# Attention's products with V in four array quadrants, and six blocks turned for the gate by transfers

## Chip, cores, metric

The kernel runs on one core of a Trainium2 chip. The metric is the device time of one launch in microseconds (us), the median of several runs; lower is better. Engines are named as in the profile: PE (TensorE's matmuls), PEld (its weight loads), DVE (VectorE), ACT (ScalarE), POOL (GpSimd) and SP (SyncE, which issues most transfers here). Matrix data are fp32, and an fp32 matmul with 65 moving columns leaves two records of each kind (LDWEIGHTS, MATMUL) in the trace.

## What is computed

Local and global attention over 4 sequences of 768 tokens with 8 heads of 64, then a mixture of 8 experts, of which each token takes two.

```python
scores = scale * q @ k.T + bias          # kept: the first 8 keys, and the 96 last ones up to the token
a = softmax(scores)                      # (B, H, S, S), masked
x = (a @ v).transpose(0, 2, 1, 3).reshape(3072, 512)
noisy = x @ w_gate + log1p(exp(x @ w_noise)) * noise
# the two best experts of each token, weighted by the softmax of their two values
out[t] += weight[t, e] * (relu(x[t] @ w1[e]) @ w2[e])
```

## The kernel before

**Attention** goes over 24 blocks of 128 tokens (`g`; six to a sequence, `i` counts them within it). A loop of 48 iterations takes four heads of a block each; `n` steps by 2, so iteration k has n = 2k and each block has two. Keys of a block are a window: 96 of the block before, 8 global ones and the block's own, and the 128 queries are dealt with in two halves `s` of 64, each with a window of 168 keys (`WIN`). The schedule is written out by hand, and each engine runs its instructions in that order. One iteration does, in this order: `score(n + 2)` (four DVE operations that read the scores' banks, four exponentials on ACT), `trans(n)` and `trans(n + 1)` (six PE transposes, two copies on ACT), in every second iteration `gate_t` of an earlier block, then `product(n + 4)` (eight PE matmuls of 64x64 weights in four quadrants of the array, rows by head, columns by `y`), `norm(n - 4)` (three DVE operations that read the PSUM bank of an earlier product with V), `attend(n - 2)` (the product with V), parts of the gate, and what is due by `todo` (loads of q, k and v three blocks ahead, w1 of the first expert split into two parts by ACT and POOL, zeroing). Iteration 10 forms the first scores of block 6, iteration 12 those of block 7.

**attend** (L859). In a block with i > 0 it has 16 matmuls in two rounds of eight. In round 0, weights of 64 rows sit at array position (0, 0) for one half of the queries and of 40 rows at (64, 64) for the other, so two quadrants work. In round 1, weights of 104 and 128 rows take the whole height, in two column halves. Each matmul moves 65 columns (64 of V and a column of ones, for the softmax's sum). One call writes one PSUM bank, and calls alternate between banks 5 and 6 (`rings`), so `norm` of one call reads a bank that the next `attend` does not write.

**V** is loaded by `load_v` (L657): `vs`, 128 rows of 2080 bytes, and for i > 0 `vp`, 96 rows of the block before and 8 global rows (the latter only in the first four uses of each sequence's buffers, as a transfer of its own).

**The gate** needs each block's x with features along the partitions. `gate_t` (L365) copies x on POOL into two planes of 16-bit halves (`halved`, four copies of 128x256), which `gate_l` (L382) has SP store to DRAM (`xd`) for the later gathers; it turns x by four PE transposes into bank 2, and ACT copies the 128x512 result into `pair` (L380). `gate_l` multiplies two blocks at a time with the gate's weights, `gate_s` brings the result into place, and `route`, a chain of small DVE steps dealt out by `tick`, chooses experts after blocks 5, 11, 16, 20 and 23.

**Experts** follow. The first begins with `turn` of its gathered tokens and `up(0, ...)`, the others run the same way, and in them tokens are turned by SP's transposing transfer and joined by ACT (`flip` L260, `weave` L269). PSUM bank tags 5 and 6 serve `down` there.

SP issues its transfers in program order.

Of the kernel before, what the change touches and what calls it, by code (L numbers as in the profile page):

```python
# [10 lines left out]
F32 = mybir.dt.float32  # L11
# [10 lines left out]
P = 128  # L22
# [13 lines left out]
def tile_local_global_attention_then_moe(  # L36
# [24 lines left out]
    NT = B * NB  # L61
    WIN = NP + NG + Q
    windowed = 1 <= n_local <= NP + 1 and 0 <= n_global <= NG
    scale = 1.0 / math.sqrt(D)
# [15 lines left out]
    turns = {}  # L80

    def bank(tag):
        ring = rings[tag]
        key = tuple(ring)
        turns[key] = turns.get(key, -1) + 1
        return psum.tile([P, 512], F32, name=tag, tag=f"b{ring[turns[key] % len(ring)]}", bufs=1)

# [271 lines left out]
    def partner(g):  # L359
# [3 lines left out]
        return (g - a) % 2  # L363

    def gate_t(g):  # L365
        x = XR.pop(g).rearrange("p h d -> p (h d)")
        stored[g] = gp.tile([P, 2 * Dm], U16, name="xt", bufs=4)
        halved(planes(stored[g]), words(x))
        ps = bank("m").rearrange("p (k t) -> p k t", k=KC)
        for k in range(KC):  # L370
            nc.tensor.transpose(ps[:, k], x[:, k * P:(k + 1) * P], ident)
        j = partner(g)
        if j is None:
            XT[g] = ys[2].rearrange("p (k t) -> p k t", k=KC)
            to = XT[g]
        else:
            if j == 0:
                XT[g + 1] = pairs[0].rearrange("p (k j t) -> p k j t", k=KC, j=2)
            to = XT[g + 1 - j][:, :, j]
        nc.scalar.activation(to, ps, AF.Copy)  # L380

    def gate_l(g):  # L382
        nc.sync.dma_start(xd[DUMP + g * P:DUMP + (g + 1) * P], stored.pop(g))
        j = partner(g)
        if j == 0:
            return
        ps = bank("m")[:, :P]
        x = XT.pop(g)
        x = [x] if j is None else [x[:, :, i] for i in range(2)]
# [243 lines left out]
    with ExitStack() as actx:  # L633
        ac = actx.enter_context(tc.tile_pool(name="ac", bufs=1))
        aw = actx.enter_context(tc.tile_pool(name="aw", bufs=2))

        qs, ks, vs, vp = {}, {}, {}, {}
# [19 lines left out]
        def load_v(g):  # L657

            b, i = divmod(g, NB)
            vs[g] = aw.tile([P, HD], F32, name="vs", bufs=4)  # L660
            nc.sync.dma_start(vs[g], v[b, i])
            if i:
                vp[g] = vpb[g % 4]
                nc.sync.dma_start(vp[g][:NP], v[b, i - 1, P - NP:])
                if i <= 4:
                    nc.sync.dma_start(vp[g][NP:], v[b, 0, :NG])

        if windowed:
            vpb = [ac.tile([NP + NG, HD], F32, name=f"vp{j}") for j in range(4)]
            pairs.append(ac.tile([P, 2 * Dm], F32, name="pair"))  # L670
# [52 lines left out]

            abuf = [ac.tile([P, 2 * WIN], F32, name=f"a{j}") for j in range(4)]
        else:
# [121 lines left out]
        def trans(n):  # L847
            g, u, b, i = geo(n)
            w = 3 * P if i else 2 * P
            ps = bank("at")[:, :w]  # L850
            x = A.pop(n)
            for k, c in enumerate((0, 2 * WIN - P, NP + NG) if i else (0, P)):
# [6 lines left out]
        def attend(n):  # L859

            g, u, b, i = geo(n)
            ps = pav[g, u // 2] = bank("av")[:, :4 * D1].rearrange("p (h d) -> p h d", h=4)
            at = [AT.pop(n + x) for x in range(2)]
            heads = [(at[x], 2 * y + x, y * Q) for x in range(2) for y in range(2)]
            parts = [[(vs[g], 0, P, 0)], [(vs[g], 0, P, 1)]]
            if i:
                parts = [[(vs[g], 0, Q, 2), (vp[g], 0, NP + NG, 0)], [(vp[g], Q, NP + NG, 2), (vs[g], 0, P, 1)]]
            n = len(parts[0])
            for k in range(n):
                for a, h, q0 in heads:  # L870
                    c = slice((u // 2 * 4 + h) * D1, (u // 2 * 4 + h + 1) * D1)
                    for s in range(2):
                        t, r, z, part = parts[s][k]
                        nc.tensor.matmul(ps[s * Q:(s + 1) * Q, h], a[r:z, part * P + q0:part * P + q0 + Q], t[r:z, c],  # L874
                                         start=k == 0 and (n == 1 or h == 0), stop=k + 1 == n,
                                         tile_position=(r, s * Q), skip_group_check=True)

        def norm(n):
# [3 lines left out]
            if u == 0:  # L882
                XR[g] = ys[g % 2].rearrange("p (h d) -> p h d", h=H)
            den = aw.tile([P, 4], F32, name="den", bufs=2)
            nc.vector.tensor_scalar(den, ps[:, :, D], 1e-9, None, op0=OP.add)
            tick(4)
            nc.vector.reciprocal(den, den)
            tick(5)
            h0 = 2 * u
# [11 lines left out]
        def whole(g):  # L901
# [20 lines left out]
            for hp in range(HP):  # L922
# [8 lines left out]
                for x in range(2):  # L931
# [13 lines left out]
                    for j in range(NB):  # L945
# [10 lines left out]
                                     den[:, :, None].to_broadcast([P, 2, D]))  # L956
            for f in gate_t, gate_l, gate_s:
                f(g)
# [20 lines left out]
        else:  # L979
# [27 lines left out]
            for n in range(0, NPAIR, 2):  # L1007
# [40 lines left out]
            for t in range(TA):  # L1048
                if t == 2:
                    gate_l(NT - 2)  # L1050
                turn(0, t, bank("sc"))
# [7 lines left out]

    rings.update(sc=[0, 1], m=[2])  # L1060
    with ExitStack() as mctx:
        mc = mctx.enter_context(tc.tile_pool(name="mc", bufs=1))
        w2h = mc.tile([P, FC, Dm], FR, name="w2h")
# [116 lines left out]
        def back(e, i):  # L1180
# [11 lines left out]

        late, last = pending
        slots = {
            0: [(late, 24)], 1: [gate_t, (late, 27)], 2: [(late, 30)], 3: [gate_l, (late, 33)],
            4: [(late, 36)], 5: [gate_s, (late, 39)], 6: [(late, 42)], 7: [(late, 45), (last, 2)],
            8: [], 9: [(late, 48), (last, 5)], 10: [(last, 7)], 11: [(last, 8)],
            12: [(late, 52), (last, 9)], 13: [(last, 12)], 14: [(last, 14)], 15: [(late, 54), (last, 16)],
            16: [(last, 19)], 17: [(last, 21)], 18: [(last, 23)], 19: [(last, 26)],
            20: [(last, 30)], 21: [(last, 33)], 22: [(late, 57), (last, 35)], 23: [(last, 37)],  # L1200
            24: [(last, 39)], 25: [(last, 42)], 26: [(late, 61)], 27: [(last, 45)],
            28: [(last, 48)], 29: [(late, 99), split], 30: [split], 31: [(last, 52)],
        }
# [290 lines left out]

    wctx.close()
    left = nc.values_load(more[0:1, E:E + 1], min_val=0, max_val=N)
    with tc.If(left > 0), tc.tile_pool(name="lc", bufs=1) as lc:
# [92 lines left out]
```

## Time and profile before

| | us |
|---|---|
| median of 3 runs (lowest, highest) | 720.09 (717.33, 720.92) |
| the profiled execution, device time | 718.65 |
| its span, first to last instruction | 716.9 |
| PE busy in the span | 692.7 |
| DVE / ACT / POOL busy | 457.1 / 440.0 / 323.3 |
| mean granted clock of PE | 0.995 of 2.4 GHz |

The profile is of one execution. "Busy" is the union of an engine's instructions; matmuls overlap in the array, so PE is busy for nearly the whole span and this alone doesn't say how well it is used. The chain of waits follows the work that ended last backwards; an operation whose share of it is large sets the time in that stretch. Attention takes roughly the first 160 us of the span.

### The profile page before, as it was taken

What the parts mean: (1) busy time and instruction counts of PE and PEld (TensorE: products, weight loads), DVE (VectorE), ACT (ScalarE), POOL (GpSimd) and SP (SyncE); (2) the same over time, 40 slices, a digit from 0 to 9 for tenths busy, and PEclk for the clock granted to TensorE, in tenths of its full rate; (3) what the DMA queues carried; (4) which work ended last, traced back from release to release, by engine and by line L of the source; (5) the groups of instructions that cost most, each with busy time, mean ns of one, the idle gap of its engine ahead of it and who ended that gap; (6) DMA issues with size and microseconds to landing.
All of it is one profiled execution on the core that took longest, in us unless ns stands there. A gap on an engine that the chain in (4) does not pass through costs nothing.

```text
span 716.9 us, 16231 instructions
## 1 busy us (share of the span) xinstructions
PE 692.7 (97%) x5769; PEld 618.3 (86%) x5769; DVE 457.1 (64%) x1473; ACT 440.0 (61%) x922; POOL 323.3 (45%) x416
## 2 busy tenths in 40 slices
PE   7999999999999799999999999999999999999995
PEld 5888888787789699999799989999899898889984
DVE  7669888977946376746564665576376756656600
ACT  6888787662437496546664685587467646755511
POOL 3363626481087362164606462644555344632222
PEclk9999999999999999999999999999999999999999
DMA  8996778685098784167916792587459547843233
GB/s 252 336 279 216 216 233 289 203 299 188 0 261 181 155 141 118 27 120 160 207 16 133 158 217 48 118 174 165 75 148 201 108 121 166 185 74 89 31 45 47
DMA packets 129913, 111.10 MB, mean 155 GB/s; under 512 B 51578, under 2 KB 96762, under 8 KB 129824
## 3 DMA queue, kind: packets, MB, share of 16 engines
q1 hardware_dynamic: 118416, 83.84, 42.9%
q0 software_dynamic: 11264, 25.89, 20.1%
q8 instruction: 47, 0.77, 0.5%
q14 instruction: 42, 0.34, 0.2%
q10 hardware_dynamic: 144, 0.26, 0.1%
HBM read 71.07 MB, written 27.59 MB: 138 GB/s over the span
## 4 chain that ended last, share of the span: by engine, by line
PE 64%; DVE 10%; issue 8%; DMA 7%; POOL 5%; ACT 5%; POOLq 0%; SPq 0%; ACTq 0%; DVEq 0%
PE bank L1397 20%; PE av L1144 19%; PE av L1167 7%; PE av L874 4%; PE sc L823 4%; PE at L853 3%; DMA xt<-xg 3%; DMA xg<-xd,ids 2%; DVE wall L196 2%; PE at L1107 1%; ACT hh L1088 1%; DVE w2l L196 1%; POOL out_dram L1120 1%; DVE ns L837 1%; DMA xd<-xt 1%
## 5 line engine op out<-in xcount | busy, mean ns | idle before, releaser
L1397 PE MATMUL bank<-xh,wall 128*128 128x384 f32 (+4 forms) x784 | 216.3, 343 | 1.1 <-ACT aside L1438 0.9
L1397 PEld LDWEIGHTS bank<-xh,wall 128*128 128x128 f32 x784 | 143.5, 188 | 6.7 <-DVE wall L196 1.4
L1397 PE MATMUL bank<-xl,wall 128*128 128x384 f32 (+4 forms) x392 | 133.4, 340 | 0.0
L1144 PE MATMUL av<-w2h,hh 128*128 128x512 f32 x304 | 120.3, 396 | 4.0 <-ACT aside L1176 2.3
L1120 POOL DMA_INDIRECT out_dram<-y,ids x40 | 63.8, 1596 | 127.7 <-ACT y L1117 124.4
L1144 PE MATMUL av<-w2h,hl 128*128 128x512 f32 x304 | 119.5, 393 | 0.3 <-DVE hl L1092 0.3
L1144 PE MATMUL av<-w2l,hh 128*128 128x512 f32 x304 | 119.1, 392 | 0.0
L196 DVE TENSOR_TENSOR wall<-raw,wall 128x512 fp32r<-128x512 f32 (+1 forms) x84 | 73.0, 875 | 48.4 <-ACT wall L195 48.3
L1092 DVE SCALAR_TENSOR_TENSOR hl<-bank,hh 128x384 fp32r<-128x384 f32 (+4 forms) x84 | 47.1, 561 | 66.5 <-ACT hh L1088 66.3
L195 ACT ACTIVATE wall<-raw 128x512 fp32r<-128x512 f32 (+1 forms) x84 | 58.0, 698 | 43.2 <-POOL raw L1252 43.2
L243 POOL DMA_INDIRECT xg<-xd,ids x53 | 58.8, 1109 | 52.1 <-DVE place L293 32.5
L840 ACT ACTIVATE a<-ns,mx 128x168 f32<-128x168 f32 (+1 forms) x192 | 67.9, 422 | 19.3 <-DVE mx L837 18.6
L1397 PEld LDWEIGHTS bank<-xl,wall 128*128 128x128 f32 x392 | 73.9, 188 | 2.7
L275 ACT ACTIVATE xg<-xt 128x1024 uint16<-128x1024 uint16 (+3 forms) x46 | 60.0, 1307 | 19.7 <-DMA xt<-xg 19.6
L1144 PEld LDWEIGHTS av<-w2h,hl 128*128 128x128 f32 x304 | 57.1, 188 | 14.1 <-DVE hl L1092 1.5
L1144 PEld LDWEIGHTS av<-w2h,hh 128*128 128x128 f32 x304 | 57.1, 188 | 14.0 <-ACT aside L1176 2.5
L1144 PEld LDWEIGHTS av<-w2l,hh 128*128 128x128 f32 x304 | 57.1, 188 | 9.3 <-DVE w2l L196 0.3
L837 DVE CUSTOM_DVE_ANT_0 ns<-sc,bias 128x168 f32<-128x168 f32 (+1 forms) x188 | 51.7, 319 | 18.4 <-PE sc L823 12.3
L1251 POOL TENSOR_TENSOR raw<-raw 128x256 f32<-128x256 f32 x28 | 21.9, 781 | 85.8 <-DVE wall L196 85.4
L874 PE MATMUL av<-vs,at 128*64 128x65 f32 (+1 forms) x768 | 57.3, 224 | 0.0
L235 POOL COPY xt<-y 128x256 uint16<-128x256 uint16 x96 | 35.2, 405 | 49.0 <-DVE y L890 46.9
L1088 ACT ACTIVATE hh<-bank 128x384 fp32r<-128x384 f32 (+4 forms) x84 | 41.8, 497 | 23.6 <-DVE bank L1467 16.0
(214 smaller groups left out, 1485.6 us busy)
## 6 DMA issues: line engine op xcount, KB each, us to landing
raw<-in_w SPq DMA_DIRECT2D x64, 256.0 KB
raw<-in_w SPq DMA_DIRECT2D x32, 512.0 KB
out_dram<-zero SPq DMA_DIRECT2D x14, 512.0 KB
vs<-in_v SPq DMA_DIRECT2D x24, 260.0 KB
xd<-xt SPq DMA_DIRECT2D x24, 256.0 KB
qbuf<-in_q SPq DMA_DIRECT2D x23, 256.0 KB
ks<-in_k SPq DMA_DIRECT2D x20, 272.0 KB
vp<-in_v SPq DMA_DIRECT2D x20, 195.0 KB
```

Of the source, the lines that this page charges most:

```text
L195: nc.scalar.activation(hi, src, AF.Copy)
L196: eng.tensor_sub(lo, src, hi.bitcast(F32))
L243: nc.gpsimd.indirect_dma_start(out=xg[e, t].bitcast(U16)[:m], out_offset=None, in_=xd[:n], in_offset=bass.IndirectOffsetOnAxis(ap=r, axis= ...
L275: nc.scalar.activation(words(x), xt.pop((e, t)).rearrange("p (h k) t -> p h (k t)", h=2), AF.Copy)
L837: nc.vector.tensor_tensor_reduce(out=ns[x][:, s, :w], in0=ps[:, s], in1=bias[:, u + x, s] if i else bias0[:, u + x, s], scale=-scale, scal ...
L840: nc.scalar.activation(A[n + x][:, s * w:(s + 1) * w], ns[x][:, s, :w], AF.Exp, bias=mx[x][:, s:s + 1], scale=-1.0)
L874: nc.tensor.matmul(ps[s * Q:(s + 1) * Q, h], a[r:z, part * P + q0:part * P + q0 + Q], t[r:z, c], start=k == 0 and (n == 1 or h == 0), stop ...
L1088: nc.scalar.activation(inner(e)[0][j][:, f, :src.shape[1]], src, AF.Relu)
L1120: ins = nc.gpsimd.indirect_dma_start(out=out, out_offset=bass.IndirectOffsetOnAxis(ap=r, axis=0), in_=y, in_offset=None, bounds_check=N + ...
L1144: nc.tensor.matmul(ps, x[j][:, f, cols], w[:, f], start=n == 0, stop=n == 3 * FC - 1)
L1167: nc.tensor.matmul(to, w[:, f, cols], x[:, f], start=n == 0, stop=n == 3 * FC - 1)
L1397: nc.tensor.matmul(ps, wb[c % 2][u][:, 2 * a + k], x[v][:, 2 * b + k], start=start and n == 0, stop=stop and n == 5, skip_group_check=True)
```

## The change

Two parts. `attend` keeps its 16 matmuls, but round 0 is dealt over four quadrants: of heads with x = 0 as before, of heads with x = 1 at (64, 0) and (0, 64). To this end the attention weights of odd heads are laid out in another order in their buffer (24 columns longer, the first 24 of them zero, by two memsets), V comes from the host in two arrangements, one for even and one for odd heads, and `vp` is a full 128-row transfer (260 KB, one transfer instead of one or two). Heads with x = 0 and x = 1 write different banks, so each call writes both banks of one tile `av` (`P, 2, 512`), in one of three column ranges in turn; `norm` reads both banks.

For blocks 0, 1, 2, 3, 8 and 9 (`LATE`), `gate_t` only makes the 16-bit planes; `store` has SP store them, and then turns them with a transposing transfer into `flipped`; `gate_w`, one block later, joins the planes on POOL (four copies of 128x256) into a tile of its own; `gate_l` follows one iteration after that, `gate_s` one later still. PE's four transposes and ACT's copy of these blocks fall away.

```diff
-                nc.sync.dma_start(vp[g][:NP], v[b, i - 1, P - NP:])
-                if i <= 4:
-                    nc.sync.dma_start(vp[g][NP:], v[b, 0, :NG])
+                nc.sync.dma_start(vp[g], v[b, i, 1])
...
+    LATE = (0, 1, 2, 3, 8, 9)
+    def gate_w(g):
+        XT[g] = gp.tile([P, Dm], F32, name="xg", bufs=7)
+        halved(words(XT[g]), flipped.pop(g).rearrange("p (h k) t -> p h (k t)", h=2))
+        XT[g] = XT[g].rearrange("p (k t) -> p k t", k=KC)
...
         halved(planes(stored[g]), words(x))
+        if late(g):
+            return
...
+    def store(g):
+        x = stored.pop(g)
+        nc.sync.dma_start(xd[DUMP + g * P:DUMP + (g + 1) * P], x)
+        if late(g):
+            flipped[g] = gp.tile([P, 2 * Dm], U16, name="xt", bufs=4).rearrange("p (c t) -> p c t", t=P)
+            nc.sync.dma_start_transpose(flipped[g], x)
...
+        av = pools["av"] = pa.tile([P, 2, 512], F32, name="av")
...
-                    nc.scalar.activation(A[n + x][:, s * w:(s + 1) * w], ns[x][:, s, :w], AF.Exp,
+                    a = (1 - s) * w + Q - GQ if x and i else s * w
+                    nc.scalar.activation(A[n + x][:, a:a + w], ns[x][:, s, :w], AF.Exp,
...
-                parts = [[(vs[g], 0, Q, 2), (vp[g], 0, NP + NG, 0)], [(vp[g], Q, NP + NG, 2), (vs[g], 0, P, 1)]]
-            n = len(parts[0])
-            for k in range(n):
-                for a, h, q0 in heads:
+            c0 = n // 2 % 3 * 2 * D1
+            ps = pav[g, u // 2] = av[:, :, c0:c0 + 2 * D1].rearrange("p x (y d) -> p x y d", y=2)
+                rounds = [
+                    [(0, 0, vs, 2, 0, Q), (0, 1, vp, 0, Q, Q), (1, 0, vp, 2, Q, GQ), (1, 1, vp, 0, 0, Q)],
+                    [(0, 0, vp, 0, 0, NP + NG), (1, 0, vs, 1, 0, P), (0, 1, vs, 1, 0, P), (1, 1, vs, 2, 0, P)],
+                ]
+            for k, parts in enumerate(rounds):
+                for y in range(2):
+                    for s, x, t, part, r, m in parts:
+                        c = ((x * 2 + u // 2) * 2 + y) * D1
+                        nc.tensor.matmul(ps[s * Q:(s + 1) * Q, x, y], at[x][r:r + m, part * P + y * Q:][:, :Q],
+                                         t[g][r:r + m, c:c + D1], start=k == 0 and y == 0,
+                                         stop=k + 1 == len(rounds),
+                                         tile_position=(r, s * Q), skip_group_check=True)
...
-            nc.vector.tensor_mul(XR[g][:, h0:h0 + 4], ps[:, :, :D],
-                                 den[:, :, None].to_broadcast([P, 4, D]))
+            to = XR[g][:, 2 * u:2 * u + 4].rearrange("p (y x) d -> p x y d", y=2)
+            nc.vector.tensor_mul(to, ps[:, :, :, :D], den[:, :, :, None].to_broadcast([P, 2, 2, D]))
...
-                if g >= 0 and odd and g not in ends:
+                if g >= 0 and odd and g not in ends and not late(g):
                     gate_s(g, True)
+                if not odd and late(g - 2):
+                    gate_s(g - 2, True)
                 if g >= 0 and not odd:
-                    gate_l(g)
+                    store(g)
+                    if not late(g):
+                        gate_l(g)
+                if not odd and late(g - 1):
+                    gate_w(g - 1)
+                if odd and late(g - 1):
+                    gate_l(g - 1)
```

## Rows read from the trace of the kernel before

**Rows 1.** Busy time by stretch: span, then PE, PEld, DVE, ACT, POOL, clock, DMA share, GB/s.
```profile
0.00:16.00 16.00, 11.04 (x142) 7.97 (x146) 11.20 (x67) 9.74 (x28) 5.62 (x27) 1.00 0.91 260
...
16.00:46.00 30.00, 29.89 (x610) 25.97 (x602) 18.90 (x117) 25.46 (x72) 13.70 (x30) 1.00 1.00 308
46.00:58.00 12.00, 11.01 (x204) 9.20 (x196) 8.81 (x50) 10.99 (x32) 8.04 (x14) 1.00 0.75 234
...
90.00:128.00 38.00, 37.80 (x733) 32.66 (x730) 33.89 (x218) 30.21 (x87) 16.86 (x36) 1.00 0.85 260
```

**Rows 2.** Chain of waits, shares by line: stretches 16:46, 46:58, 58:90, 90:128, 128:161.
```profile
by line: PE av L874 36.8%; PE at L853 24.8%; PE sc L823 23.1%; PE m L371 5.8%; PE m L393 3.9%; DVE ns L837 3.3%; ACT a L840 1.5%; issue 0.7%; PE lg L409 0.6%; DVE den L885 0.3%; DVE tab L758 0.2%; DVE mx L837 0.1%; ACTq L855 0.1%
by line: ACT a L840 20.9%; DVE ns L837 12.8%; ACT at L855 10.8%; issue 7.4%; PE at L853 6.7%; PE sc L823 6.7%; DVE y L890 6.4%; PE m L393 5.4%; DVE aside L465 4.7%; ACT pair L380 4.1%; DVE aside L458 3.6%; ACT xh L195 3.2%; DVE aside L460 2
by line: PE av L874 27.9%; PE sc L823 20.7%; PE at L853 19.1%; PE m L371 5.5%; PE m L393 5.4%; PE lg L608 5.2%; DVE ns L837 4.9%; issue 1.5%; DVE aside L465 1.3%; DVE aside L471 1.2%; PE lg L528 1.2%; DVE aside L481 1.2%; DVE aside L479 1.1
by line: PE av L874 23.5%; PE at L853 17.2%; PE sc L823 16.5%; DVE ns L837 8.8%; PE m L371 4.6%; PE lg L608 4.4%; PE m L393 4.0%; DVE y L890 2.9%; DVE aside L465 2.9%; issue 2.2%; PE lg L406 1.1%; DVE aside L460 1.0%; DVE aside L471 1.0%; P
by line: DMA xd<-xt 24.6%; POOL wall L555 18.5%; issue 10.1%; POOL xt L235 8.8%; POOL xg L243 7.2%; PE av L874 3.6%; DVE ns L837 3.1%; DVE y L890 2.6%; DVE aside L481 2.2%; PE sc L823 2.1%; PE m L393 1.7%; POOL xg L235 1.5%; DVE aside L479 
```

**Rows 3.** Chain of waits in order of time: start us, us, what.
```profile
0.81 3.93 DMA ks<-in_k
...
34.87 1.08 PE av L874 x32
...
36.75 0.44 PE m L371 x4
37.19 0.60 PE sc L823 x16
...
43.15 0.73 PE sc L823 x16
```

**Rows 4.** Timeline of PE, single matmuls of one attend, and six small ones: start us, us.
```profile
34.74 0.22 PE L874 MATMUL av<-vs,at 64*64 64x65 f32 x1
...
34.80 0.22 PE L874 MATMUL av<-vs,at 64*64 64x65 f32 x1
...
35.37 0.22 PE L874 MATMUL av<-vp,at 104*64 104x65 f32 x1
...
35.38 0.22 PE L874 MATMUL av<-vs,at 128*64 128x65 f32 x1
...
35.43 0.22 PE L874 MATMUL av<-vp,at 104*64 104x65 f32 x1
...
67.90 0.29 PE L530 MATMUL lg<-aside,ones 128*128 128x8 bf16 x6
```

**Rows 5.** Timeline of SP's issues: start us, us of issuing.
```profile
0.81 0.46 SPq L649 DMA_DIRECT2D ks<-in_k  x1
...
26.40 1.42 SPq L652 DMA_DIRECT2D qbuf<-in_q  x1
...
35.80 1.49 SPq L652 DMA_DIRECT2D qbuf<-in_q  x1
```

**Rows 6.** Instructions that touch tile xt: count, minimum, median, maximum in ns.
```profile
L235 POOL COPY xt<-y x96: 390/403/437, 13.8 to 163.0; 128x256 uint16<-128x256 uint16 x96
L267 SPq DMA_TRANSPOSE xt<-xg x46: 1178/1254/4086, 205.1 to 621.6; - x46
```

**Rows 7.** ACT's groups by line from 16 to 46 us.
```profile
L380 ACT ACTIVATE pair<-m 128x512 f32<-128x512 f32 x5 | 3.0, 602 | 0.0
```

**Rows 8.** Timeline of PE and DVE: start of an attend, norm's last read (two cases).
```profile
52.54 0.22 PE L874 MATMUL av<-vs,at 64*64 64x65 f32 x1
...
53.25 0.41 DVE L890 TENSOR_TENSOR y<-av,den 128x256 f32<-128x256 f32 x1
...
122.48 0.43 DVE L890 TENSOR_TENSOR y<-av,den 128x256 f32<-128x256 f32 x1
...
122.68 0.34 PE L874 MATMUL av<-vs,at 128*64 128x65 f32 x4
```

More of the change, by code (lines that the diff above doesn't have):

```diff
@@ L85, in bank @@
         turns[key] = turns.get(key, -1) + 1
-        return psum.tile([P, 512], F32, name=tag, tag=f"b{ring[turns[key] % len(ring)]}", bufs=1)
+        b = ring[turns[key] % len(ring)]
+        if b in AV and "av" in pools:
+            return pools["av"][:, AV.index(b)]
+        return pools.get(b, psum).tile([P, 512], F32, name=tag, tag=f"b{b}", bufs=1)
     xd = dram.tile([N + DUMP, 2 * Dm], U16, name="xd")
@@ L363, in partner, with late @@
         return (g - a) % 2
+    LATE = (0, 1, 2, 3, 8, 9)
+    flipped = {}
+    def late(g):
+        return windowed and g in LATE
+    def gate_w(g):
+        XT[g] = gp.tile([P, Dm], F32, name="xg", bufs=7)
+        halved(words(XT[g]), flipped.pop(g).rearrange("p (h k) t -> p h (k t)", h=2))
+        XT[g] = XT[g].rearrange("p (k t) -> p k t", k=KC)
     def gate_t(g):
@@ L387, in gate_l @@
         ps = bank("m")[:, :P]
-        x = XT.pop(g)
-        x = [x] if j is None else [x[:, :, i] for i in range(2)]
+        if late(g):
+            x = [XT.pop(g - 1), XT.pop(g)]
+        else:
+            x = XT.pop(g)
+            x = [x] if j is None else [x[:, :, i] for i in range(2)]
         for i, y in enumerate(x):
@@ L635, in tile_local_global_attention_then_moe @@
         aw = actx.enter_context(tc.tile_pool(name="aw", bufs=2))
+        pa = actx.enter_context(tc.tile_pool(name="pa", bufs=1, space=bass.MemoryType.PSUM))
+        av = pools["av"] = pa.tile([P, 2, 512], F32, name="av")
         qs, ks, vs, vp = {}, {}, {}, {}
@@ L722, in tile_local_global_attention_then_moe @@
             biases(bias0, dist0, range(H))
-            abuf = [ac.tile([P, 2 * WIN], F32, name=f"a{j}") for j in range(4)]
+            abuf = [ac.tile([P, 2 * WIN + j % 2 * (Q - GQ)], F32, name=f"a{j}") for j in range(4)]
+            for j in 1, 3:
+                nc.gpsimd.memset(abuf[j][:, :Q - GQ], 0.0)
         else:
@@ L851, in trans @@
             x = A.pop(n)
-            for k, c in enumerate((0, 2 * WIN - P, NP + NG) if i else (0, P)):
+            if n % 2 and i:
+                parts = [Q - GQ + NP + NG, Q - GQ + WIN + GQ, 0]
+            else:
+                parts = [0, 2 * WIN - P, NP + NG] if i else [0, P]
+            for k, c in enumerate(parts):
                 nc.tensor.transpose(ps[:, k * P:(k + 1) * P], x[:, c:c + P], ident)
@@ L861, in attend @@
             g, u, b, i = geo(n)
-            ps = pav[g, u // 2] = bank("av")[:, :4 * D1].rearrange("p (h d) -> p h d", h=4)
             at = [AT.pop(n + x) for x in range(2)]
-            heads = [(at[x], 2 * y + x, y * Q) for x in range(2) for y in range(2)]
-            parts = [[(vs[g], 0, P, 0)], [(vs[g], 0, P, 1)]]
+            c0 = n // 2 % 3 * 2 * D1
+            ps = pav[g, u // 2] = av[:, :, c0:c0 + 2 * D1].rearrange("p x (y d) -> p x y d", y=2)
+            rounds = [[(s, x, vs, s, 0, P) for x in range(2) for s in range(2)]]
             if i:
-                parts = [[(vs[g], 0, Q, 2), (vp[g], 0, NP + NG, 0)], [(vp[g], Q, NP + NG, 2), (vs[g], 0, P, 1)]]
-            n = len(parts[0])
-            for k in range(n):
-                for a, h, q0 in heads:
[L871 to L875, printed above, removed]
+                rounds = [
[9 more added lines that the diff above has]
+                                         stop=k + 1 == len(rounds),
                                          tile_position=(r, s * Q), skip_group_check=True)
@@ L883, in norm @@
                 XR[g] = ys[g % 2].rearrange("p (h d) -> p h d", h=H)
-            den = aw.tile([P, 4], F32, name="den", bufs=2)
-            nc.vector.tensor_scalar(den, ps[:, :, D], 1e-9, None, op0=OP.add)
+            den = aw.tile([P, 2, 2], F32, name="den", bufs=2)
+            nc.vector.tensor_scalar(den, ps[:, :, :, D], 1e-9, None, op0=OP.add)
             tick(4)
@@ L956, in whole @@
                                      den[:, :, None].to_broadcast([P, 2, D]))
-            for f in gate_t, gate_l, gate_s:
+            for f in gate_t, store, gate_l, gate_s:
                 f(g)
@@ L1060, in tile_local_global_attention_then_moe @@
     rings.update(sc=[0, 1], m=[2])
+    del pools["av"]
     with ExitStack() as mctx:
+        pm = mctx.enter_context(tc.tile_pool(name="pm", bufs=1, space=bass.MemoryType.PSUM))
+        pools.update({b: pm for b in AV})
         mc = mctx.enter_context(tc.tile_pool(name="mc", bufs=1))
@@ L1570 @@
     vx[..., :D] = v.transpose(0, 2, 1, 3).reshape(B, NB, P, H, D)
+    if 1 <= int(inputs["n_local"]) <= NP + 1 and 0 <= int(inputs["n_global"]) <= NG:
+        v0 = vx.reshape(B, NB, P, H // 4, 2, 2, D + 1).transpose(5, 0, 1, 2, 3, 4, 6).reshape(2, B, NB, P, -1)
+        half = P // 2
+        vx = np.zeros((B, NB, 2, P, 2, v0.shape[-1]), v.dtype)
+        vx[:, :, 0, :, 0] = v0[0]
+        vx[:, 0, 0, :, 1] = v0[1][:, 0]
+        vx[:, 1:, 0, half:, 1] = v0[1][:, 1:, :half]
+        vx[:, 1:, 1, :half, 1] = v0[1][:, 1:, half:]
+        first = [np.broadcast_to(x[:, :1, :NG], (B, NB - 1, NG, x.shape[-1])) for x in v0]
+        before = [np.concatenate([x[:, :-1, P - NP:], y], axis=2) for x, y in zip(v0, first)]
+        vx[:, 1:, 1, :NP + NG, 0] = before[0]
+        vx[:, 1:, 1, half:, 1] = before[1][:, :, :half]
+        vx[:, 1:, 0, 2 * half - NP - NG:half, 1] = before[1][:, :, half:]
+        vx = vx.reshape(B, NB, 2, P, -1)
+    else:
+        vx = vx.reshape(B, NB, P, -1)
     arrays = {
```

29 lines of the change are left out of this document (16 added, 13 removed).

## Prediction

> **What bounds the kernel now.** I read busy times by stretch first, then the chain of waits in the same stretches, then single operations of the chain, then SP's issues. From 16 to 46 us PE is busy for 29.89 of 30 us, and the chain there is PE's almost alone: products with V 36.8%, transposes, scores, and the gate's transposes 5.8% [rows 1, 2]. The reader should see in the same row that the transfers are at their limit as well: DMA share 1.00, 308 GB/s; from 0 to 16 us it is 0.91 [rows 1]. From 46 to 58 us the chain passes to ACT and DVE, which have fallen behind. From 58 to 128 us it is PE's again, but from 90 on about a quarter is DVE's (scores, and the small steps of the routing), and DVE is busy for 33.89 of 38 us [rows 1, 2]. From 128 to 161 us the chain is POOL's masks and copies and the gathers' transfers; products with V hold 3.6% of it [rows 2]. So only work before about 128 us can be shortened on PE with an effect, and how far depends on DMA early and on DVE later. The experts after 161 us are untouched and should only shift.
>
> **Products with V.** One attend holds 1.08 us of PE for 32 records [rows 3]. In round 0 a quadrant starts its next record 57 ns after the last (34.74, 34.80), which is also the pace of a column half in round 1 (35.37, 35.43) [rows 4]. 16 records in two quadrants are 8 steps: 8 x 57 = 0.46 us. In four quadrants they are 4 steps, 0.23 us, if quadrants run beside each other. The scores already do that: 16 records of 128 columns hold 0.60 us [rows 3], while a 128-column pass costs 0.11 us (four gate transposes, 0.44 us [rows 3]), so that two at a time would be 8 x 0.11 = 0.88. Upper bound of the gain 0.23 us. Lower bound: small full-array matmuls start 25 ns apart (six in 0.29 us, the last about 0.17 us long [rows 4]); if every start needed 25 ns, 16 would take 0.40 and the gain would be 0.06 us. But two column halves start 10 ns apart (35.37, 35.38 [rows 4]). I take 0.23. There are 20 blocks with i > 0 and two calls each: 40 x 0.23 = 9.2 us of PE work. Round 1, the switch of shape between rounds and DVE's reads keep their counts; the two memsets on POOL come early, when it waits.
>
> The Trainium skill (TensorE: Matmul & The Clock Gate, "Wait — 56ns, not 53.3ns?") says that starts of matmuls never come closer than about 25 ns. The full-array row agrees, the two column halves do not; by the rule the 9.2 us would be 2.4.
>
> **The gate's blocks.** Six times 0.44 us of PE [rows 3] is 2.6 us, and ACT loses six copies of 0.6 us [rows 7]. Added: POOL's four copies of 0.40 us [rows 6], six times 1.6 = 9.7 us, in a stretch in which POOL is busy 13.70 of 30 us [rows 1]; and six transposing transfers, which SP issues in 1.25 us each at the median [rows 6], ahead of the loads of q, k and v that follow in its program.
>
> **What these transfers delay.** I take SP's queue as first in, first out. Through the issue of block 6's q at 26.40 us there are 38 transfers (37 on SP, one on ACT; first and last in [rows 5]), by their shapes 9.40 MB. Moved by 16 us: 16 x 260 GB/s = 4.16 MB; the remaining 5.24 MB at 308 GB/s [rows 1] take until 33.0 us, and a transfer needs 2 to 3 us beyond its bytes (the first took 3.93 us for 0.28 MB [rows 3], of which the bytes are 0.9). So this q lands at 35 to 36 us. Iteration 10 uses it at 37.19 [rows 3]: 1 to 2 us of slack. For block 7 (46 transfers, 11.51 MB, the last issued at 35.80 [rows 5]) the same gives 39.9 + 2 to 3, for a use at 43.15 [rows 3]: about 1. I use 1.5 for both.
>
> Before block 7's q the change puts three transposing transfers and five larger loads of V. One transposing transfer of 0.26 MB costs the queue 0.85 us if it moves at the stretch's 308 GB/s [rows 1], and 1.25 us if SP's issuing sets its pace [rows 6]; nothing would need idle capacity, and the share of 1.00 leaves none. I take 1.0. The loads of V add 0.26 MB, 0.85 us. Together 3.85 us (3.4 to 4.6). So these scores start 3.85 - 1.5 = 2.3 us later than now, although PE, with ten cheaper attends (2.3 us) and four blocks' gate transposes (1.8 us), would be 4 us ahead: PE's gain here turns into a wait for q. The gate of blocks 2 and 3 comes next, in iteration 13: it needs the fourth transposing transfer and then 1.6 us of POOL, and PE waits behind it, up to 1.5 us. Against that, ACT has four copies of 0.6 us less, and ACT held the chain from 46 us on [rows 2]; I credit 2 us. Stage up to 58 us: 2.3 + 1.2 - 2.0 = +1.5 us. Bounds: -1.5 (the transfers cost nothing, and PE gains only the slack) and +4.6.
>
> **From 58 to 128 us.** Products with V hold 27.9% of 32 us and 23.5% of 38 us, 8.9 us each [rows 2], that is 8.3 attends each; 16.5 x 0.23 = 3.8, and the gate of blocks 8 and 9 0.9: -4.7 us.
>
> Against this, a new wait. Now norm reads one bank while the next attend writes the other. With both banks in each call, attend must wait for norm's last read, if an access by two engines to one bank has to be kept apart (the kernel's alternation of banks suggests it). In nine of the 24 iterations from 52 to 127 us attend begins before that read ends, by 0.11 to 1.12 us and 3.8 us together (first: 52.54 against 53.25 + 0.41; last: 122.68 against 122.91 [rows 8]). Behind the waiting attend stand the next transposes on PE, for which ACT waits. Nothing is lost where the order on DVE leaves attend behind norm anyway. Bounds 0 and 3.8; I take half, 1.9, because PE waits for DVE in these iterations in other places too. Stage: -4.7 + 1.9 = -2.8 us (-4.7 to 0).
>
> The Trainium skill (PSUM — Partial Sum Buffer, "PSUM bank collisions raise a hardware error") wants two engines kept apart by bank and group of 32 partitions, not by address; the rows above show overlap only on different banks. Without that rule the stage would be -4.7.
>
> **From 128 us.** Ten attends save 2.3 us of PE, and about one of them is on the chain [rows 2]; waits for norm may cost as much. 0 (-1 to +0.5).
>
> **Sum.** +1.5 - 2.8 + 0 = -1.3 us on 718.65 us of the profiled execution: 717.3. That execution is 1.4 us under the median, so as a median of several runs it may be 718.7; I predict 717.5. Differences under 0.5% (3.6 us) are about what a measurement of this kernel can't tell from no change.
>
> **Rivals.**
> *PE stays the bound throughout.* The transfers fit in, no wait for norm. For it: PE's share of the chain up to 46 us, and that q is asked for only as it is needed. Against it: DMA share 1.00. Early -4.1, later -4.7, tail -0.5: 709.4 us. Half of it, with q late but the later stage whole, gives 713 to 714. Chance of faster than 0.5%: 0.36.
> *The queue decides, and it is slower.* The place is iteration 12's scores and iteration 13's gate. If the transposing transfer holds the queue for SP's 1.25 us and the gate's wait is whole, +4.6, while later stages give -0.9: 722.4 us. Slower by over 0.5% needs a transfer of about 1.2 us or more in the queue. Chance 0.17.
> *Quadrants don't run beside each other* (25 ns for each start): attends save 0.06 us; of the 3.8 in the later stage 1.0 is left: 720.1 us. Chance 0.07, within "same". That rule of the skill, named above, would bring it about.
> *The forecast*, 717.5 us, alone 714.5 to 721.0: 0.40.
> So faster 0.36, same 0.47, slower 0.17. The range that leaves out 2 in 10 is 709.5 to 723.5.
>
> **What would show it.** Right: attend near 0.85 us with four starts within some 30 ns; PE idle before the scores of iterations 10 or 12, released by q or k; POOL waiting for the transposing transfer and PE's gate matmuls for POOL in iteration 13; attend released by norm in iterations with routing; ACT less on the chain from 46 to 58 us. Wrong: no PE wait for q and iteration 14 earlier than 48 us by 3 us or more (then the first rival), or attends still at 1.0 us (the third). My least certain price is what a transposing transfer costs a full queue.

## The result, and the profile after

| | before | after |
|---|---|---|
| median of 4 runs, us (lowest, highest) | 718.81 (717.33, 720.92) | 726.83 (725.43, 728.18) |
| profiled execution, us | 718.65 | 727.89 |
| its span, us | 716.9 | 726.1 |
| mean granted clock | 0.995 | 0.990 |

The ratio is 1.0118, with a 95% interval of 1.0086 to 1.0151: slower by 8 us, outside the forecast's range and on its other side.

Busy times of after, by stretch (columns as in [rows 1]; lines of the kernel have moved: attend is L912, scores L855, norm L929, the gate's product L423, POOL's plane copies L242, the transposing transfer L408).

```profile
16.00:46.00 30.00, 24.76 (x501) 20.30 (x492) 16.84 (x106) 23.12 (x64) 13.57 (x35) 0.94 1.12 304
38.00:40.00 2.00, 2.00 (x54) 1.87 (x54) 1.16 (x10) 0.86 (x3) 0.00 (x0) 0.82 1.12 362
40.00:42.00 2.00, 2.00 (x22) 1.67 (x24) 0.46 (x2) 1.56 (x5) 0.00 (x0) 0.50 1.23 191
42.00:44.00 2.00, 2.00 (x46) 1.81 (x39) 1.39 (x11) 1.55 (x6) 0.00 (x0) 0.83 1.18 308
46.00:58.00 12.00, 10.64 (x186) 7.78 (x186) 5.47 (x34) 6.88 (x20) 10.31 (x18) 1.00 1.00 275
58.00:90.00 32.00, 29.39 (x595) 23.53 (x598) 29.61 (x181) 24.17 (x69) 17.67 (x37) 1.00 0.79 223
90.00:128.00 38.00, 36.88 (x751) 29.99 (x747) 30.79 (x195) 28.36 (x81) 18.67 (x42) 1.00 0.81 256
```

Against [rows 1], PE from 16 to 46 us has 5.1 us less to show, and works at a mean granted clock of 0.94. The transfers' engines are busier (1.12 against 1.00) for no more bytes (304 against 308 GB/s); a share above 1 means that packets of several transfers overlap on an engine. From 58 on PE is idle for 2.6 and 1.1 us: work was taken from it, and the time was not.

PE's timeline in after, where it stood still longest (start, length, in brackets the idle time before and what ended it).

```profile
37.88 0.68 PE L855 MATMUL sc<-ks,qbuf 64*64 64x128 f32 x13 [2.62 <-DMA qbuf<-in_q]
...
39.70 1.54 PE L890 MATMUL at<-ident,a 128*128 128x128 f32 x6
41.18 1.13 PE L855 MATMUL sc<-ks,qbuf 64*64 64x128 f32 x16
...
46.18 0.88 PE L855 MATMUL sc<-ks,qbuf 64*64 64x168 f32 x14 [1.80 <-DMA qbuf<-in_q]
```

The scores of iterations 10 and 12 wait for q, 2.62 and 1.80 us. After the first wait the granted clock falls to 0.50, the 1.2 GHz level (40 to 42 us), and six transposes take 1.54 us. Next, from 48 us on, the gate, and one attend:

```profile
49.83 0.43 PE L423 MATMUL m<-xg,wgn 128*32 128x128 f32 x8
50.64 1.57 PE L423 MATMUL m<-xg,wgn 128*32 128x128 f32 x8 [0.39 <-POOL xg L242]
52.14 0.87 PE L890 MATMUL at<-ident,a 128*128 128x128 f32 x6
...
55.63 0.64 PE L423 MATMUL m<-pair,wgn 128*32 128x128 f32 x16 [0.74 <-ACT pair L401]
...
58.99 0.27 PE L912 MATMUL av<-vs,at 64*64 64x65 f32 x1 [1.04 <-DVE y L929]
59.00 0.28 PE L912 MATMUL av<-vp,at 64*64 64x65 f32 x3
59.10 0.22 PE L912 MATMUL av<-vs,at 64*64 64x65 f32 x1
59.11 0.23 PE L912 MATMUL av<-vp,at 64*64 64x65 f32 x3
```

The 16 gate products of blocks 2 and 3 hold PE for 2.38 us (49.83 to 52.21), because their operand arrives piece by piece from POOL; those of a pair turned by PE take 0.64 (55.63). Six transposes at full clock take 0.87. The attend shows four quadrants starting within 0.02 us, and the next four 0.11 later. It waited 1.04 us for norm, whose last read ends at 58.94:

```profile
58.53 0.41 DVE L929 TENSOR_TENSOR y<-av,den 128x256 f32<-128x256 f32 x1
```

POOL joins block 3 only then, four copies in a row:

```profile
50.11 1.64 POOL L242 COPY xg<-xt 128x256 uint16<-128x256 uint16 x4
```

The table of waits of after from 0 to 170 us (engine and line, what it waited for: us in all, times, longest):

```profile
POOL xg L242 <- DMA xt<-xt: 12.0, 3, 6.8
PEld av L912 <- DVE y L929: 10.5, 22, 1.4
...
PE sc L855 <- DMA qbuf<-in_q: 4.4, 2, 2.6
...
PE av L912 <- DVE y L929: 4.0, 9, 1.0
...
PEld m L423 <- POOL xg L242: 2.6, 9, 0.7
```

The weight loads' waits and the matmuls' waits for norm overlap, so they are not added. In before, over the same 170 us, attend's loads waited for DVE's division once:

```profile
PEld av L874 <- DVE den L887: 0.2, 1, 0.2
```

In after POOL stands up to 6.8 us for a transposing transfer.

SP's issues in after, and its transfers' median from issue to landing from 16 to 46 us:

```profile
17.44 1.60 SPq L408 DMA_TRANSPOSE xt<-xt  x1
...
26.85 2.34 SPq L408 DMA_TRANSPOSE xt<-xt  x1
...
31.29 1.56 SPq L684 DMA_DIRECT2D qbuf<-in_q  x1
...
38.08 2.08 SPq L408 DMA_TRANSPOSE xt<-xt  x1
...
40.82 0.50 SPq L684 DMA_DIRECT2D qbuf<-in_q  x1
```

```profile
qbuf<-in_q SPq DMA_DIRECT2D x4, 256.0 KB, 5.2
...
xt<-xt SPq DMA_TRANSPOSE x4, 7.0
```

The q of blocks 6 and 7 are issued at 31.29 and 40.82, 4.9 and 5.0 us later than in [rows 5]. The three transposing transfers ahead of block 7's take SP 1.60, 2.34 and 2.08 us to issue.

### The profile page after: what moved, and what is told of

Its sections match the earlier page's. It is cut to its first block, busy times and chain, and to the rows that moved or that the text cites. A ratio compares the mean times of both kernels' runs of the same rounds, so it can differ in the third digit from the quotient of the medians.

```text
span 726.1 us, 16177 instructions
## 1 busy us (share of the span) xinstructions
PE 691.0 (95%) x5745; PEld 608.4 (84%) x5745; DVE 458.6 (63%) x1473; ACT 437.1 (60%) x916; POOL 331.7 (46%) x442
## 4 chain that ended last, share of the span: by engine, by line
PE 43%; issue 9%; DMA 7%; DVE 7%; ACT 5%; POOL 4%; POOLq 0%; SPq 0%; ACTq 0%; DVEq 0%
PE bank L1447 17%; PE av L1194 17%; PE av L1217 6%; DMA xt<-xg 4%; DMA xg<-xd,ids 3%; DVE wall L203 2%; ACT hh L1138 2%; POOL out_dram L1170 1%; DVE w2l L203 1%; PE at L1157 1%; ACT wall L202 1%; POOL raw L1302 1%; PE sc L1157 1%; PE bank L1240 1%; POOL xg L250 1%
## 5 line engine op out<-in xcount | busy, mean ns | idle before, releaser
L242 POOL COPY xt<-y 128x256 uint16<-128x256 uint16 x96 | 34.9, 401 | 46.6 <-DVE y L929 40.9
L855 PE MATMUL sc<-ks,qbuf 64*64 64x168 f32 (+1 forms) x752 | 43.4, 317 | 11.6 <-DMA ks<-in_k 5.3
```

## Experiments

Theory A (queue): the transposing transfers hold the transfers' engines longer than their bytes, and q comes late. Theory B (tile): with both banks in each call, attend waits for norm, and that takes back what the quadrants gain. Rival C: the loss comes from POOL's joins, which are late and hold up the gate. The table lists the start of attend's first matmul in some iterations, minus the same in before, from one profiled execution each; "ratio" is that of the run's times to those of before on the same chip, with its 95% interval (it can differ a little from the quotient of the two medians).

| kernel | it. 9 | 12 | 17 | 23 | 31 | 37 | 48 | ratio |
|---|---|---|---|---|---|---|---|---|
| before, start in us | 34.69 | 43.70 | 58.91 | 78.49 | 103.52 | 122.68 | 157.84 | |
| after | -2.45 | +3.07 | +6.84 | +5.67 | +7.79 | +7.42 | +7.51 | 1.0118 (1.0086 to 1.0151) |
| V part alone | -0.77 | +0.22 | +1.78 | +1.20 | +1.35 | +0.99 | +2.77 | 1.0015 (0.9991 to 1.0039) |
| double tile alone | -0.36 | -0.36 | +1.20 | +1.36 | +2.34 | +2.94 | +5.64 | 1.0088 (1.0055 to 1.0121) |
| gate part alone | -1.41 | +3.34 | +6.96 | +5.91 | +8.09 | +8.09 | +8.09 | 1.0135 (1.0064 to 1.0206) |
| transfers unread | +0.09 | +5.09 | +5.91 | +5.91 | +6.17 | +6.16 | +6.15 | 1.0081 (1.0045 to 1.0116) |
| plain copies unread | -0.50 | -0.50 | -0.51 | -0.50 | -0.51 | -0.51 | +1.01 | 1.0000 (0.9974 to 1.0026) |
| on ACT's queue | +1.75 | +8.96 | +9.44 | +9.43 | +9.69 | +9.69 | +9.69 | 1.0113 (1.0069 to 1.0157) |
| blocks 8 and 9 alone | +0.17 | +0.18 | +0.17 | -0.87 | +1.28 | +1.27 | +1.27 | 0.9998 (0.9973 to 1.0023) |
| before, loads moved by 28 | -0.02 | -0.13 | -1.71 | -2.06 | +2.09 | +2.09 | +2.08 | 1.0015 (0.9977 to 1.0053) |
| after, same | -0.93 | -0.64 | +0.01 | -1.16 | +5.87 | +5.50 | +5.58 | 1.0096 (1.0060 to 1.0133) |
| gate part, same | -1.44 | -1.20 | -1.25 | -2.63 | +3.97 | +3.97 | +5.55 | 1.0057 (1.0026 to 1.0089) |
| before, loads moved by 48 | -0.02 | -0.13 | -1.71 | -2.06 | -2.07 | -0.73 | +2.78 | 1.0042 (1.0019 to 1.0066) |
| blocks 0 to 3, same | -1.58 | -1.58 | -2.19 | -2.53 | -2.27 | -0.93 | +4.19 | 1.0056 (1.0029 to 1.0084) |
| after, blocks 0 to 3, same | -1.24 | -0.96 | -0.28 | -0.86 | -0.71 | +2.31 | +7.46 | 1.0151 (1.0105 to 1.0196) |

### The parts alone

The V part alone is the changed kernel with no block turned by transfers:

```diff
-    LATE = (0, 1, 2, 3, 8, 9)
+    LATE = ()
```

> The four-quadrant products with V alone; all blocks turned for the gate by PE as before. Queue theory (the early transposing transfers delay q and k) with bank theory (attend waits for norm's reads and so gives its gain back): no transposing transfer is left, so iterations 10 and 12 start within 1 us of before, and the end is within 3 us of before. If the queue alone explains the loss and the wait for norm is free: 5 to 9 us faster than before. If the products with V themselves are the loss: 6 to 8 us slower.

Measured 719.7 us against 717.49. Its waits from 0 to 170 us:

```profile
PEld av L912 <- DVE y L929: 11.7, 21, 1.8
PE av L912 <- DVE y L929: 5.4, 10, 1.6
```

No difference that can be measured: neither faster nor slower. The gate part alone is before with `LATE`, `store`, `gate_w` and the new order of the gate's steps, and before's attend and V:

```diff
+    LATE = (0, 1, 2, 3, 8, 9)
...
+            nc.sync.dma_start_transpose(flipped[g], x)
...
+                if not odd and late(g - 1):
+                    gate_w(g - 1)
```

> The six blocks turned by transfers alone; products with V as before, in alternating banks. Queue theory: scores of iterations 10 and 12 wait for q by 1 to 3 us, the gate of iteration 13 for POOL, and the end is 3 to 6 us slower than before. Rival (the turned blocks cost nothing, the whole loss is the wait for norm): 1 to 3 us faster than before.

Measured 727.53 us against 717.49, more than the 3 to 6 us expected: this part alone has the loss. Waits from 30 to 62 us:

```profile
POOL xg L235 <- DMA xt<-xt: 10.0, 2, 5.8
...
PE sc L846 <- DMA qbuf<-in_q: 5.1, 2, 4.1
```

### What in each part costs

The double tile alone keeps two quadrants in round 0 and before's V; only the output goes to both banks of one tile in each call:

```diff
-            ps = pav[g, u // 2] = bank("av")[:, :4 * D1].rearrange("p (h d) -> p h d", h=4)
+            c0 = n // 2 % 3 * 2 * D1
+            ps = pav[g, u // 2] = av[:, :, c0:c0 + 2 * D1].rearrange("p x (y d) -> p x y d", y=2)
...
-                        nc.tensor.matmul(ps[s * Q:(s + 1) * Q, h], a[r:z, part * P + q0:part * P + q0 + Q], t[r:z, c],
+                        nc.tensor.matmul(ps[s * Q:(s + 1) * Q, x, y], a[r:z, part * P + y * Q:part * P + y * Q + Q],
```

> Products with V in two quadrants as before, same loads, same gate, but each attend writes both banks of one tile. Bank theory: attend is released by norm in the iterations with routing, 3 to 8 us slower than before. Rival (norm is early enough, as in the iterations without routing): within 1.5 us of before.

Measured 723.77 us against 717.49. Its waits from 0 to 170 us:

```profile
PEld av L884 <- DVE y L900: 9.8, 20, 1.6
...
PE av L884 <- DVE y L900: 3.9, 8, 1.3
```

The tile alone costs 6.3 us; with the quadrants and their V the loss is 2.2. So the quadrants do gain, about 4 us by these medians (the two intervals do not overlap), and the tile takes it: B holds.

Transfers unread is before with the six transposing transfers in their places, into tiles that nobody reads; the blocks are still turned by PE:

```diff
...
+        if windowed and g in (0, 1, 2, 3, 8, 9):
+            unread = gp.tile([P, 2 * Dm], U16, name="xt", bufs=4).rearrange("p (c t) -> p c t", t=P)
+            nc.sync.dma_start_transpose(unread, x)
```

> The kernel before plus the same six transposing transfers, into tiles that nobody reads; PE's transposes stay. Queue theory: q of blocks 6 and 7 lands 3 to 6 us later against about 2 us of slack, 1 to 4 us slower than before at iteration 12, some of it kept to the end. Rival (POOL, which joins the planes and blocks on the transfers, is the cause): within 1 us of before.

Measured 723.86 us against 717.49. From 30 to 62 us:

```profile
PE sc L827 <- DMA qbuf<-in_q: 4.7, 2, 3.5
```

The transfers alone cost 6.4 us, with nothing joined and only POOL waiting once for one of them, 0.6 us, for a buffer: A holds, and C is not needed for the larger part. At iteration 12 they are 5.1 us late, above the 1 to 4 expected. C is not nothing: after iteration 12 the gate part loses another 3.6 us (3.34 to 6.96), the unread transfers 0.8. Then the same with plain copies of the same bytes:

```diff
-            nc.sync.dma_start_transpose(unread, x)
+            nc.sync.dma_start(unread, x)
```

> The kernel before with six extra transfers at the places of the six transposing ones, of the same bytes, but plain copies, not read by anybody. Theory that any transfer in the full queue delays q by its bytes: about as slow as the six transposing ones were, +0.6% to +0.8%. Theory that the transposing form is what costs: +0.1% to +0.4%, with each a queue entry of 0.7 us against 1.7.

Measured 718.93 us against 719.9: nothing. It is the transposing form that costs. What its packets take of the engines could be read when ScalarE issued the six on a queue of its own (`nc.scalar.dma_start_transpose`):

> The kernel before with the six transposing transfers that nobody reads, issued by ScalarE on its own queue instead of SP's. Theory that the order in SP's queue delays q: q no longer waits behind them, within 0.3% of before apart from six issues on ScalarE of 1.3 us each (0 to +3 us). Theory that the transfer itself holds the engines that all queues share: q is late as before, +0.5% to +0.9%.

Measured 727.05 us against 719.12. Queues from 16 to 46 us, and then ScalarE's queue from 0 to 110 us (packets, MB, share of 16 engines' time):

```profile
q1 hardware_dynamic: 8372, 7.01, 85.0%
q10 hardware_dynamic: 3168, 0.79, 26.0%
```

```profile
q10 hardware_dynamic: 6480, 1.84, 14.3%
```

The last one holds six transposing transfers and one plain load (ACT's first of q, from DRAM), which stands alone in that queue in the run with plain copies, from 0 to 110 us:

```profile
q10 hardware_dynamic: 144, 0.26, 1.0%
```

So 6336 packets are six transfers, 13.3% of 110 us, 2.4 us of the 16 engines each; from 16 to 46 us, 3168 packets are three, 26.0% of 30 us, 2.6 us each. That plain load of the same bytes took 1.0% of 110, 1.1 us. Packets overlap, so this is packet time and not time taken from the others. The run's time itself decides nothing on the order in SP's queue: PE waited for q there only once after the start, 0.2 us, and ACT stood behind its own issue.

```profile
45.34 1.81 ACTq L387 DMA_TRANSPOSE xt<-xt  x1
47.20 0.28 ACT L400 ACTIVATE aside<-m 128x128 f32<-128x128 f32 x1 [4.50 <-issue]
```

SP's issue of block 7's q in that run tells more:

```profile
41.80 0.99 SPq L656 DMA_DIRECT2D qbuf<-in_q  x1
```

It is 6.0 us later than in [rows 5], with no transposing transfer in SP's own queue. This speaks for the engines that the queues share, and against SP's time to issue as the only reason; but SP waited 2.9 us for a transposing transfer there too, by the profile, and ACT and PE were late, so the two are not told apart.

### Does a turned block pay where the queue is clear?

Blocks 8 and 9 alone, with transfers after 50 us:

```diff
-    LATE = (0, 1, 2, 3, 8, 9)
+    LATE = (8, 9)
```

> The gate's part alone, for blocks 8 and 9 only, whose transfers are issued after the queue has drained (from 50 us on). Queue theory: a transposing transfer costs nothing there, so within 0.3% of before, 0 to -1 us (two blocks' turns, 0.9 us of TensorE). Theory that a turned block costs wherever it stands (GpSimd's join, the gate's wait): 0.2% to 0.4% slower.

Measured 719.05 us against 718.9. At iteration 23 it is 0.87 us ahead, as two blocks' turns should give, and from there to iteration 31 it loses 2.1. PE, and then POOL, in that stretch:

```profile
84.97 1.89 PE L416 MATMUL m<-xg,wgn 128*32 128x128 f32 x16
...
90.16 0.64 PE L416 MATMUL m<-pair,wgn 128*32 128x128 f32 x16
```

```profile
80.87 3.97 POOL L578 TENSOR_SCALAR wall<-iota_p,aside 128x128 fp32r<-128x128 f32 x6
84.79 1.62 POOL L235 COPY xg<-xt 128x256 uint16<-128x256 uint16 x4
```

The join of block 9 stands behind 3.97 us of POOL's routing matrix, and the gate's 16 products run at POOL's pace, 1.89 us, where those of a block pair turned by PE take 0.64. That is C, of 1.3 us for these two blocks; the other 0.9 of the 2.1 was not traced.

Next, other early transfers were moved out of the way: the emptied rows by 16, and the first expert's weights with their splits by 28 in `n`, which counts two to an iteration (the expectations call these 28 iterations; they are 14).

```diff
-            at(12, empty_rows)
+            at(28, empty_rows)
...
-                at(8 + 2 * j, load_w)
+                at(36 + 2 * j, load_w)
...
-                at(16 + 2 * j, split, 0, 1, j // 2 + j % 2 * NU, nc.gpsimd)
+                at(44 + 2 * j, split, 0, 1, j // 2 + j % 2 * NU, nc.gpsimd)
```

Before with this move, as the control:

> The kernel before, with its early transfers that nobody needs soon (the rows that are emptied, the router's weights, the split of later rows) issued 28 iterations later, so that the queue is less full when q and k of iterations 8 to 13 are asked for. The control for the next two runs. Queue theory: the kernel before already had 1.5 us of slack at iteration 12, so this gains little: within 0.3% of before, 0 to -2 us. Theory that the moved transfers matter where they land later: +1 to +3 us.

The changed kernel with it:

> The changed kernel with the same early transfers moved 28 iterations later. Queue theory: the score products of iterations 10 and 12 no longer wait for q (2.6 and 1.8 us before), TensorE's granted clock stays at 1.00 between 38 and 44 us, and the kernel comes back to within -0.5% to +0.4% of before, where the double tile's waits keep it. Rival, that the turned blocks lose by GpSimd's joins or by the wait of the gate for them: it stays 0.7% to 1.2% slower, with no wait for q.

The gate part with it:

> The gate's part alone (six blocks turned by transfers, joined by GpSimd; attention as before), with the same early transfers moved 28 iterations later. Queue theory: 0.1% to 0.7% faster than before (2.6 us of TensorE's turns saved, no wait for q). Rival, joins or the gate's wait for them: 0.4% to 1% slower, with TensorE waiting for the joined rows at iterations 7 to 13.

Measured 720.09, 728.21 and 723.68 us against 718.9. By the medians the rival's number came: after is still 1% slower, although no score product waits for q any more, apart from the very first, which does in before as well. The table says where. At iteration 23 the changed kernel is 0.9 us behind its control, where without the move it was 5.7 behind; so up to there A is right. Between iterations 23 and 31 the control itself loses 4.2 us and the changed kernel 7.0. There the splits stand right behind POOL's routing matrix. A second place, loads at `56 + 2 * j` and splits at `64 + 2 * j`, and turned blocks 0 to 3 alone:

> Control: the kernel before with the weights' loads at iterations 29 to 32 and their splits at iterations 33 to 40 instead of 5 to 8 and 9 to 16, and the emptied rows 8 iterations later. In the first move (loads at 19 to 22, splits at 23 to 30) the kernel was 2 us ahead at iteration 24 and lost 4 us from 25 to 31, where GpSimd built the routing matrix beside the splits. If that was the place, this one keeps the 2 us: -0.4% to +0.1%. If the splits cost wherever they lie: 0 to +0.4%.

> Blocks 0 to 3 alone turned by transfers (8 and 9 lost by GpSimd's late joins), attention as before, with the same move. Queue theory: four blocks' turns saved, 1.8 us of TensorE, and no wait for q: 0 to -2 us against before_far. Theory that a turned block never pays: +1 to +4 us against before_far.

> The changed kernel with blocks 0 to 3 alone turned and the same move. If the parts add up: gate_far plus what the V part alone gave (0 to +1 us). Rival, that the double tile's waits are paid more when TensorE is less idle elsewhere: 2 us or more above gate_far.

Measured 722.09, 723.4 and 728.35 us against 719.12. The control keeps its 2 us until iteration 31 and then loses 4.8, from iteration 34 to 40, where the splits now stand: in both places the loss falls on the splits, and not on the weights' loads ahead of them. The turned blocks are 0.2 us ahead of the control at iteration 31, of 1.8 us of turns taken from PE, and 1.4 behind at 48: they do not pay here, and they hardly cost (the two intervals overlap widely). The two parts together do not add up: 5 us more than the gate's part, while the V part alone was 2.2 us off before. Why this is so stays open.

### The tile's wait, removed by order

In the V part alone, `norm(n - 4)` was issued ahead of `score(n + 2)`, then between its two head pairs, and, as a control, ahead of it in before:

```diff
+                if n >= 4:
+                    norm(n - 4)
                 if n + 2 < NPAIR:
                     score(n + 2)
...
-                if n >= 4:
-                    norm(n - 4)
```

> The V part alone (quadrants, double tile; no turned blocks), with the division of iteration n issued on VectorE ahead of the next iteration's scores instead of behind them, so that the double tile is read earlier. Double-tile theory: the waits of the products with V for the division (17 us in the V part alone) fall below 5 us and the quadrants' gain appears, 0.5% to 1.2% faster than before (4 to 8 us). Rival, that the chain behind the scores (exponentials, transposes) sets the pace and not the tile: the division ahead of the scores makes these 0.7 us later in each iteration, and the kernel is 0 to 1% slower than the V part alone.

> The same, with the division between the scores of the two head pairs of an iteration, half way. Double-tile theory: waits for the division fall by half, 0.2% to 0.8% faster than before. Rival, the chain behind the scores: within 0.3% of the V part alone.

> Control: the kernel before, with the division ahead of the scores. Its products with V hardly waited for the division, so the order can gain nothing by the tile: double-tile theory 0 to +0.6% (scores 0.7 us later where VectorE is the limit). If it gains as much as the V part does, the order itself was the gain and not the tile.

Measured 766.26, 740.4 and 768.14 us against 719.9, ratios 1.0667 (1.0625 to 1.0709), 1.0284 (1.0252 to 1.0316) and 1.0677 (1.0643 to 1.0710). All my expectations fell. Attend no longer waits for norm, but DVE waits for attend, and its scores behind it; waits from 0 to 200 us of the V part and of before in this order:

```profile
DVE den L924 <- PE av L912: 58.3, 40, 3.2
```

```profile
DVE den L885 <- PE av L874: 61.0, 39, 3.3
```

With the division ahead of the scores DVE stood for PE in 40 and 39 iterations. Half way between the scores it did so for 7.5 us in all, and most of that run's 20 us stays unexplained. The order as it was is worth far more than the tile's wait. A second double tile, the other way to take that wait away, needs two more PSUM banks and was not tried. None of these kernels beat before by more than the measurement can tell.

## Why the prediction was wrong, step by step

The failed step is **what these transfers delay**: the price of a transposing transfer in the full queue, taken at 1.0 us from bounds of 0.85 and 1.25. Measured, its packets take 2.4 to 2.6 us of the 16 engines. Three at 1.0 less the slack of 1.5 would have made the scores of iteration 12 late by 1.5 us; the unread transfers, which change nothing else, made its attend late by 5.09. The upper bound was SP's median time to issue one among the experts (the same row of [rows 6] goes up to 4.09 us); the three issues that mattered took 1.60, 2.34 and 2.08. Whether SP or the engines set that pace is not shown. The Trainium skill (Advanced Engine Details and Errata, "X-Bar Transpose (TRN2)") holds transposing transfers to be as fast as regular ones; these runs differ, 0.26 MB in 2.4 us against 1.1 us, and the measurement decides. With packet time as the price the step's sum would have been 3 x 2.4 + 0.85 = 8.1 us in place of 3.85, and that is too much: q of block 7 was issued 5.0 us later. The rows don't show what absorbed the rest; from 40 to 42 us packets took 1.23 of the engines' time, so some of it is overlap. The mechanism was as forecast: PE 2.45 us ahead at iteration 9, then waiting for q in iterations 10 and 12, with the scores of iteration 12 starting 3.0 us later (46.18 against 43.15 [rows 3]) where 2.3 was forecast.

This step is not the whole miss. The last attend was forecast 1.3 us early and starts 7.51 late; of these 8.8 us, 5.3 fall before 58 us and 3.4 from 58 to 128.

**Up to 58 us** the forecast was +1.5, and the start of iteration 17 is 6.84 late. Up to iteration 12 it is 3.07, and that needs nothing but the transfers, as the unread ones show. After it 3.8 us more were lost, where I had +1.2 and a relief of 2.0 through ACT. Of these, 2.07 fall between the attends of iterations 13 and 14 (3.00 to 5.07 late), where the unread transfers lose nothing (6.79 to 6.55): there the gate's products of blocks 2 and 3 take 1.7 us more than a pair turned by PE (2.38 against 0.64). Another 1.38 fall between 14 and 15 (5.07 to 6.45), where the double tile alone and the V part alone lose 1.17 each: that is the first wait for norm, 1.04 us, which I had counted in the next stage. The relief did not appear. ACT has indeed 2.3 us less work before 46 us, but its inputs come late, and from 46 to 58 us it is busy for 6.88 us against 10.99. The clock's fall, which I had not counted, costs about 0.7 us in the six transposes at 39.70 alone; PE then waited 1.80 us for q, so that cost went into this wait.

**Products with V.** The length is right: from iteration 13 on an attend takes 1.03 to 1.08 us from first start to last end against 1.26 to 1.52 in before, so 0.23 saved or more, and the four starts within 0.02 us put the third rival out. The Trainium skill (TensorE: Matmul & The Clock Gate, "Wait — 56ns, not 53.3ns?") has starts at least about 25 ns apart; these rows differ, for starts in separate quadrants of the array, and the measurement decides.

**From 58 to 128 us** the forecast was -2.8, measured +0.6 (6.84 at iteration 17, 7.42 at 37). The double tile alone loses 1.7 us there (1.20 to 2.94), which looks like the 1.9 taken for the wait for norm; but that stood for nine iterations from 52 us on, and over these it loses 3.3 (-0.36 at iteration 14 to 2.94 at 37), near the bound of 3.8. That 1.7 is near 1.9 is luck. The quadrants gained less: the V part alone moves by -0.8, so they gave 2.5 of 3.8, if the two add up. And blocks 8 and 9 lost 1.1 (0.17 to 1.27) where I had them gain 0.9, because POOL was late. The V part's -0.8 and these blocks' +1.1 sum to +0.3, near the +0.6 of the changed kernel. I had looked at POOL's busy share in the early stretch only, and not at the routing matrix that stands ahead of the join.

The Trainium skill (PSUM — Partial Sum Buffer, "PSUM bank collisions raise a hardware error") keeps two engines apart by bank. The trace agrees as far as it goes: in after, an attend starts 0.05 us after norm's last read. What happens without that wait no run here shows.

**From 128 us** I set the savings against the waits, 0. The double tile loses 2.7 us there (2.94 to 5.64) and the V part 1.8, but after, 0.1. Behind attention the span is longer by another 1.7 us (9.2 in all against 7.51), of which the medians show 0.5; I have not followed that.

**The rivals.** "The queue decides, and it is slower" was the right mechanism with its condition met (1.2 us or more for a transfer); its 722.4 us was too low, since the stage to 58 us came out 2.2 us above its bound of +4.6 and the later stages gave nothing. I had given it 0.17, because I took a median issue time from another stage for an upper bound.

## What to carry to other kernels

Before moving work from a busy engine to transfers, price the transfer's form, and not its bytes alone, by the time that its packets take of the transfer engines: a plain copy into a tile that nobody reads costs one run and tells the one from the other. Work moved to an idle engine has to be on time there, so look at what stands ahead of it in that engine's order at that very moment, not at its busy share. An output tile that spans all the banks of its double buffer turns a buffer into a wait, and reordering the reader to remove that wait can cost much more than the wait.

## What the runs showed of the hardware

The packets of a transposing transfer of 256 KB (1056 of them) took 2.4 to 2.6 us of the 16 transfer engines, those of a plain load of the same bytes (144) 1.1. In after PE's granted clock was 0.50 (1.2 GHz) between 40 and 42 us, after an idle time of 2.62 us before 37.88, and it was back at 1.00 from 46 us on. Four quadrants of the array took matmuls of 65 columns with starts within 0.02 us. An attend was 0.23 us shorter or more with round 0 in four quadrants.
